# Linear attention and two mixtures on one core: the first mixture in pairs of experts, the first block of the second by plain products

## The chip, the cores and the metric

The kernel runs on one core of a Trainium2 chip. The metric is device time in microseconds (us) for one launch. TensorE (PE) multiplies, VectorE (DVE), ScalarE (ACT) and GpSimd (POOL) work on elements, and SyncE (SP) issues most of the DMAs. Every engine runs its own queue in order and waits on semaphores of the others.

## The reference, cut to what matters

Three layers follow one another on 2304 tokens of 512 numbers, in float32:

```python
def phi(x):                                  # linear attention, per head
    proj = x @ w_phi; proj -= abs(proj).max(-1, keepdims=True)
    return concatenate([exp(proj), exp(-proj)], -1)
x = phi(q) @ (phi(k).T @ v) / (phi(q) @ phi(k).sum(0) + 1e-6)

logits = x @ phi_moe                         # first mixture: 8 experts x 4 slots
slot_input = softmax(logits, over tokens).T @ x
slot_out[e] = relu(slot_input[e] @ w1[e]) @ w2[e]
x = softmax(logits, over slots) @ slot_out

P = exp(x @ w_gate - max)                    # second mixture, 8 experts
for _ in range(8):
    P /= P.sum(1) + 1e-9; P /= P.sum(0) + 1e-9; P *= N / E
out = sum(P[:, e] * (relu(x @ w1[e]) @ w2[e]) for e in range(8))
```

## The kernel before

All instructions are issued through `InOrder`, so the order of the program text is the order of each engine's queue, and every row of a trace shows line 51. Weights are loaded in units of 1 MB (four a first-mixture expert: `moe_w1` twice, `moe_w2` twice), SP issuing them in the order of the text into the pools `wa`, `wb` and `wq` (three units of 1 MB). A load waits until the tile that it overwrites has been read.

**First mixture.** For each expert e, `up(e, n)` (n = 0, 1; 16 matmuls each into `ph`) makes the hidden values of all slots, ACT writes `hid` from `ph`, `turn(e)` transposes it on PE (`pt`, two matmuls) and DVE writes the relu into `hz`, which POOL has cleared, and `down(e)` (16 matmuls) adds to `po`. The loop puts half the `up` of the next expert ahead of the `turn` and the other half behind it. Between them stand `slot_split` (DVE) and `slot_turn` (`pc` on PE, `ct` on ACT), which turn the slot weights of the tokens. After the loop `os` and `sot` are copied from `po` and `p_sot`.

**Second mixture.** The second layer's input is never formed: `make_stack` takes `sot` through `w1` (`ps`, `pr`, `st`), and `first_layer` makes the hidden values of a block of 256 tokens as `z` from `ct` and `st`. A block then multiplies a 2 x 2 split of the hidden values (a11, a12, a21, a22) with a 2 x 2 split of `w2` (b11, b12, b21, b22) by seven products of sums (`PRODUCTS`), twelve matmuls of 128x256 each, since each operand is split into a high part (`hh`, `w_hi`) and a low part (`hl`, `w_lo`), and `take` puts `x`, `y` or `z` into `xo`. ACT makes the high parts, DVE the low parts of a's (`hl_a`) and the sums s1 to s4 (`s`), POOL the low parts of the sums (`hl_s`) and those of the weights. Sums of weights are t1 to t4 (`w_sum`). In the trace `w_b` is an operand b11, b21 or b22, `w_t` one of t1 to t4. For expert 0 these operands are made during the loop of the first mixture (on ACT and DVE, from e = 5) and directly ahead of block 0 (on ACT and POOL). `sinkhorn` (`plog`, `gm`, `pgm`, `P`, `rs`, `cs`, `pcs`) makes P beside the products of expert 0: `SINK_0` and `SINK` say after which product k how many of its steps come. `pgm<-gm,ones` spreads the maximum over the partitions, `pcs` sums the columns.

The order within a block is: product k, `take`, after k = 2 the next block's `first_layer`, a step of `hidden` (the operands of the next block), weight work, steps of `sinkhorn`. The buffers of the sums (`s`) are three and go round, so `s4` waits until `hl_s` of `s1` has been read out of its buffer's earlier owner, and `s3` for `s2`'s.

## Time and profile before

| | us |
|---|---|
| median of 3 runs (lowest, highest) | 997.11 (996.86, 997.58) |
| the profiled execution's own time | 997.75 |
| its span, first to last instruction | 995.6 |
| PE busy in the span | 982.8 (99%) |
| DVE, POOL, ACT busy | 689.0, 595.0, 556.8 |
| DMA | 88.85 MB, 89 GB/s in the mean |

PE is busy 99% of the span, so time is won or lost in PE's own work and in the little that it waits. 2.15 us lie outside the span. The first mixture runs from 171 to 208 us, blocks 0 and 1 of the second from 215.67 to 238.86. The mean busy share says nothing on a single stage: DMA is near full from 175 to 222 us and almost idle in the second half.

### The profile page before, as it was taken

To read this page: it belongs to the slowest core of one execution; us is meant where nothing else is said; L and a number is where in the kernel's file an instruction comes from. 1 tells how busy PE (TensorE), PEld (TensorE's weight loads), DVE (VectorE), ACT (ScalarE), POOL (GpSimd) and SP (SyncE) were. 2 spreads that over 40 slices of the span, in tenths; PEclk is the share of its full clock that TensorE was granted. 3 is DMA by queue.
4 is the path that set the end of the run, shared out by engine and by line. 5 is a ranking of instruction groups with operands and counts; after the bars stand their busy time and mean duration, and the time that the engine had idled before them with its cause. 6 is when DMAs were issued, how large, how long until landed. Compare 5 with 4: busy or idle time off the path is not lost.

```text
span 995.6 us, 28041 instructions
## 1 busy us (share of the span) xinstructions
PE 982.8 (99%) x11698; PEld 934.5 (94%) x11698; DVE 689.0 (69%) x1359; ACT 556.8 (56%) x1018; POOL 595.0 (60%) x467
## 2 busy tenths in 40 slices
PE   8999999999999999999999999999999999999998
PEld 7899887469999999999999999999999999999998
DVE  6777776277886766676766776676676677667675
ACT  5576564266657666655564555555654655556452
POOL 2122221045678677867786688678677777687443
PEclk9999999999999999999999999999999999999999
DMA  8667577980003100310040005000300220001111
GB/s 259 209 213 235 158 261 271 392 327 2 1 1 128 44 1 2 129 43 1 1 164 8 1 2 170 1 2 28 143 2 1 76 95 1 2 1 36 51 44 64
DMA packets 28942, 88.85 MB, mean 89 GB/s; under 512 B 3856, under 2 KB 6800, under 8 KB 23056
## 3 DMA queue, kind: packets, MB, share of 16 engines
q1 hardware_dynamic: 19984, 68.05, 19.5%
q10 hardware_dynamic: 8640, 18.88, 5.9%
q8 instruction: 92, 1.51, 0.6%
q14 instruction: 34, 0.28, 0.1%
q0 software_dynamic: 192, 0.13, 0.1%
HBM read 82.33 MB, written 4.72 MB: 87 GB/s over the span
## 4 chain that ended last, share of the span: by engine, by line
PE 95%; DVE 1%; DMA 1%; ACT 1%; issue 1%; DVEq 0%; ACTq 0%
PE x L51 39%; PE y L51 20%; PE z L51 16%; PE kvacc L51 4%; PE num L51 4%; PE pq L51 2%; PE pk L51 2%; PE ut L51 2%; PE ps L51 2%; DMA moe_w<-in_moe_w 1%; PE ph L51 1%; PE po L51 1%; PE xt L51 1%; PE xl L51 1%; PE lg L51 0%
## 5 line engine op out<-in xcount | busy, mean ns | idle before, releaser
L51 POOL TENSOR_TENSOR hl_s<-s,hh_s 128x512 fp32r<-128x512 f32 x286 | 365.7, 1300 | 205.6 <-ACT hh_s L51 188.9
L51 PE MATMUL x<-w_t,hh_s 128*128 128x256 f32 x1152 | 204.9, 278 | 0.1
L51 ACT ACTIVATE hh_s<-s 128x512 fp32r<-128x512 f32 x287 | 174.7, 630 | 50.8 <-PE x L51 25.0
L51 ACT ACTIVATE r<-z 128x512 f32<-128x512 f32 x143 | 85.9, 601 | 163.7 <-PE z L51 163.1
L51 PEld LDWEIGHTS x<-w_t,hh_s 128*128 128x128 f32 x1152 | 173.5, 188 | 1.1 <-ACT xo L51 0.3
L51 DVE SCALAR_TENSOR_TENSOR xo<-x,P,xo 128x256 f32<-128x256 f32 x252 | 120.8, 479 | 69.2 <-PE x L51 68.6
L51 ACT ACTIVATE hh_a<-z 128x512 fp32r<-128x512 f32 x216 | 122.1, 600 | 72.8 <-DVE s L51 71.3
L51 PE MATMUL x<-w_t,hl_s 128*128 128x256 f32 x576 | 158.8, 277 | 0.0
L51 DVE SCALAR_TENSOR_TENSOR s<-z,r 128x512 f32<-128x512 f32 x143 | 98.0, 685 | 84.8 <-ACT hh_a L51 81.2
L51 DVE SCALAR_TENSOR_TENSOR hl_a<-z,hh_a 128x512 fp32r<-128x512 f32 x216 | 147.0, 681 | 2.7 <-ACT hh_a L51 2.7
L51 PEld LDWEIGHTS x<-w_t,hl_s 128*128 128x128 f32 x576 | 107.9, 188 | 0.0
L51 PE MATMUL z<-w_b,hh_a 128*128 128x256 f32 x576 | 102.4, 278 | 0.0
L51 PE MATMUL x<-w_t,hh_a 128*128 128x256 f32 x576 | 101.9, 277 | 0.0
L51 PE MATMUL y<-w_b,hh_s 128*128 128x256 f32 x576 | 101.8, 277 | 0.0
L51 PE MATMUL y<-w_t,hh_s 128*128 128x256 f32 x576 | 101.8, 276 | 0.0
L51 PE MATMUL x<-w_b,hh_a 128*128 128x256 f32 x576 | 101.5, 277 | 0.0
L51 DVE SCALAR_TENSOR_TENSOR s<-z,s 128x512 f32<-128x512 f32 x143 | 97.7, 683 | 3.7 <-POOL hl_s L51 2.2
L51 PEld LDWEIGHTS z<-w_b,hh_a 128*128 128x128 f32 x576 | 86.7, 188 | 2.9 <-issue 2.9
L51 PEld LDWEIGHTS x<-w_t,hh_a 128*128 128x128 f32 x576 | 86.8, 188 | 0.0
L51 PEld LDWEIGHTS y<-w_t,hh_s 128*128 128x128 f32 x576 | 86.9, 188 | 0.0
L51 PEld LDWEIGHTS y<-w_b,hh_s 128*128 128x128 f32 x576 | 86.8, 188 | 0.0
L51 PEld LDWEIGHTS x<-w_b,hh_a 128*128 128x128 f32 x576 | 86.7, 188 | 0.0
(206 smaller groups left out, 1983.5 us busy)
## 6 DMA issues: line engine op xcount, KB each, us to landing
moe_w<-in_moe_w SPq DMA_DIRECT2D x45, 1024.0 KB, 6.2
moe_w<-in_moe_w ACTq DMA_DIRECT2D x48, 256.0 KB, 3.6
moe_w<-in_moe_w ACTq DMA_DIRECT2D x12, 512.0 KB, 5.5
vs<-in_vb SPq DMA_DIRECT2D x20, 256.0 KB, 4.3
kt<-in_kT SPq DMA_DIRECT2D x18, 256.0 KB, 4.3
qt<-in_qT SPq DMA_DIRECT2D x18, 256.0 KB, 4.3
...
```

What stands on the lines that cost most here:

```text
L51: return lambda *args, **kwargs: self.tc.keep_in_program_order(make(*args, **kwargs))
```

## The change

- The pool `wq` becomes eight half units of 512 KB (`space`); `load_halves` places units 5, 6, 10 and 16 in them, so that one unit more is fetched ahead. The order of the later loads changes: the last units of the first mixture come ahead of the second mixture's.
- The first mixture goes by pairs of experts: four halves of `up`, one `turn` of four transposes, two `down`. The pool `mp` goes; `hid`, `hz` and `cst` take space in `const` and `early`. The load of `rep` is moved behind the loop.
- The operands of expert 0 for the second mixture are made no longer during the first mixture, but directly ahead of block 0 and, by `direct_work`, during it.
- Block 0 of expert 0 uses eight plain products (`DIRECT`: four results, two products each, of the a's with b11, b12, b21, b22) instead of the seven; b12 is an extra operand (`w0_b12`). Their results are copied to `xo` by ACT. `SINK_0` is moved to {0: 1, 5: 1, 6: 1, 7: 4}, so that the maximum is spread after the seventh product and the first `pcs` comes after the second product of block 1.

```diff
-    wq_cm = tc.tile_pool(name="wq", bufs=3, side="left", reuse_waits="tile")
+    wq_cm = tc.tile_pool(name="wq", bufs=1, side="left", reuse_waits="tile")
...
-    load_units(wq, 5, 6, 10)
+    space = [wq.tile([128, FF], F32, tag=f"h{n}", name=f"half{n}") for n in range(8)]
+
+    def load_halves(u, *where):
+        name, e, n = units[u]
+        unit_t[units[u]] = [space[m] for m in where]
+        for k, m in enumerate(where):
+            SP.dma_start(out=space[m], in_=a[name][e, :, n * 2048 + k * FF:n * 2048 + (k + 1) * FF])
+
+    load_halves(5, 0, 7)
+    load_halves(6, 1, 2)
+    load_halves(10, 3, 4)
     load_in_x(7)
+    load_halves(16, 5, 6)
...
-    for e in range(E):
-        if e + 1 < E:
-            up(e + 1, 0)
-        turn(e)
...
-        if e == 5:
-            w_begin(0)
-            w_hi(0, 0)
-            w_lo(0, 0, V)
-            w_sum(0, 0, V)
-        if e == 6:
-            w_lo(0, 3, V)
-            w_sum(0, 1, V)
-        if e == 7:
-            w_hi(0, 2)
-            w_lo(0, 1, V)
-            w_lo(0, 2, V)
-            w_sum(0, 3, V)
-            w_sum(0, 2, V)
...
+    for n in range(4):
+        up(n // 2, n % 2)
...
+    for p in range(E // 2):
+        a1, b1, more = 2 * p, 2 * p + 1, 2 * p + 2 < E
+        turn(p)
+        if p:
+            next(slot_turns)
+            next(slot_splits)
+        if more:
+            clear(p + 1)
+            up(a1 + 2, 0)
+            up(a1 + 2, 1)
+            if p == 0:
+                load_units(wb, 28)
+            up(b1 + 2, 0)
+            up(b1 + 2, 1)
...
+        if p == 2:
+            load_munits(3)
+        down(a1)
...
+        down(b1)
+        if p == 1:
+            load_units(wb, 31)
+            load_munits(1)
...
+    w_begin(0)
+    w_part(0, 0)
...
-            (G if i or name != "s1" else V).tensor_tensor(out=l, in0=s, in1=h.bitcast(F32), op=ALU.subtract)
+            G.tensor_tensor(out=l, in0=s, in1=h.bitcast(F32), op=ALU.subtract)
...
+    DIRECT = [
+        ("a11", 0, 0, 0), ("a11", "b12", 0, 1), ("a21", 0, 1, 0), ("a21", "b12", 1, 1),
+        ("a12", 1, 0, 0), ("a12", 5, 0, 1), ("a22", 1, 1, 0), ("a22", 5, 1, 1),
+    ]
...
+        if i == 0:
+            name, part, r, c = DIRECT[k]
+            if k < 4:
+                sums[r, c] = acc_tile(f"c{r}{c}")[:, 0:256]
+            h, l = hop[i, name]
+            accumulate(sums[r, c], h, l, wop[e, part], k < 4, k < 1 or k in (2, 4))
+            if k >= 4:
+                A.copy(out=xo[:, r, c * 256:(c + 1) * 256], in_=sums.pop((r, c)))
+            return
...
-    SINK_0 = {1: 1, 3: 1, 4: 1, 5: 1, 6: 3}
+    SINK_0 = {0: 1, 5: 1, 6: 1, 7: 4}
+
+    def direct_work(k):
+        if k == 1:
+            w_hi(0, 1)
+            w_hi(0, 5)
+            w_lo(0, 1)
+            w_sum(0, 1, V)
+            w_lo(0, 5, V)
+        if k == 2:
+            w_sum(0, 2, V)
+            w_part(0, 3)
+            w_sum(0, 3, V)
+        if k in (4, 5, 6):
+            w_part(0, {4: 2, 5: 4, 6: 6}[k])
```

PE in the first mixture before, experts 1 and 2, is one `up` half, a `turn`, the other half, a `down`:

```order
L51 MATMUL ph_3784<-moe_w_2_0_1379,sit_3676 32x256 x8
L51 MATMUL pt_3793<-ident,hid_3770 128x128 x2
L51 MATMUL ph_3784<-moe_w_2_1_1562,sit_3691 32x256 x8
L51 MATMUL po<-moe_w_1_0_3612,hz_3760 32x512 x4
L51 MATMUL po<-moe_w_1_1_0_3616,hz_3760 32x512 x2
L51 MATMUL po<-moe_w_1_1_1_3618,hz_3760 32x512 x2
```

After, PE has the second pair's transposes, both experts' `up` of the pair behind it, and then the pair's `down`:

```order
L51 MATMUL pt_3843<-ident,hids 128x128 x4
L51 MATMUL pc_3851<-ident,cst_3758 128x128 x4
L51 MATMUL ph_3864<-half_3615,sit_3686 32x256 x4
L51 MATMUL ph_3864<-half_3616,sit_3686 32x256 x4
L51 MATMUL ph_3864<-moe_w_4_1_3736,sit_3701 32x256 x8
L51 MATMUL ph_3882<-moe_w_5_0_2940,sit_3686 32x256 x8
L51 MATMUL ph_3882<-moe_w_5_1_3048,sit_3701 32x256 x8
L51 MATMUL po<-half_3613,hz_3777 32x512 x2
L51 MATMUL po<-half_3614,hz_3777 32x512 x2
L51 MATMUL po<-moe_w_2_1_2125,hz_3777 32x512 x4
L51 MATMUL po<-moe_w_3_0_2353,hz_3777 32x512 x4
L51 MATMUL po<-moe_w_3_1_2538,hz_3777 32x512 x4
```

The `turn` stands once for two experts, straight behind the `down` before it, and a half of `up` stands no longer between `hid` and it.

DVE from the maximum of the logits on, in block 0 before (`xo` is the result, `s_1_4314` and `s_1_4330` are s1 and s2 of block 1):

```order
L51 TENSOR_REDUCE gm<-plog 128x1
L51 SCALAR_TENSOR_TENSOR s_1_4314<-z_0_1_4304,r_1_4309 128x512
L51 SCALAR_TENSOR_TENSOR s_1_4330<-z_0_1_4304,s_1_4314 128x512
L51 SCALAR_TENSOR_TENSOR hl_a_1_4313<-z_0_1_4304,hh_a_1_4311 128x512
L51 TENSOR_REDUCE gm<-pgm 1x1
L51 TENSOR_TENSOR xo<-x_4240,xo 128x256
```

DVE after, at the same place (`t_4074` is t2, `w_b_4231` the low part of b22, the next two are `w_sum` 2 and 3, then s1, s2, two `hl_a` and s4 of block 1):

```order
L51 TENSOR_REDUCE gm<-plog 128x1
L51 TENSOR_TENSOR t_4074<-moe_w_0_0_3920,moe_w_0_1_3982 128x1024
L51 TENSOR_TENSOR w_b_4231<-moe_w_0_1_3982,w_b_4231 128x1024
L51 TENSOR_TENSOR moe_w_0_0_3920<-moe_w_0_0_3920,moe_w_0_1_3982 128x4x256
L51 TENSOR_TENSOR moe_w_0_1_3982<-moe_w_0_1_3982,t_4074 128x4x256
L51 SCALAR_TENSOR_TENSOR s_1_4282<-z_0_1_4272,r_1_4277 128x512
L51 SCALAR_TENSOR_TENSOR s_1_4297<-z_0_1_4272,s_1_4282 128x512
L51 SCALAR_TENSOR_TENSOR hl_a_1_4281<-z_0_1_4272,hh_a_1_4279 128x512
L51 SCALAR_TENSOR_TENSOR hl_a_1_4301<-z_0_1_4267,hh_a_1_4299 128x512
L51 SCALAR_TENSOR_TENSOR s_1_4330<-z_0_1_4267,s_1_4297 128x512
L51 TENSOR_REDUCE gm<-pgm 1x1
```

Four operations of 128x1024 moved in ahead of s1, and s4 ahead of the maximum over the partitions.

POOL after, from block 0 on (low parts of b21 and t1, then in turn `hl_s` of block 1 and a low part of a weight; before, all three low parts that POOL makes stand ahead of block 0's `hl_s`):

```order
L51 TENSOR_TENSOR w_b_4229<-moe_w_0_1_3982,w_b_4229 128x1024
L51 TENSOR_TENSOR w_t_4250<-moe_w_0_0_3920,w_t_4250 128x1024
L51 TENSOR_TENSOR hl_s_1_4304<-s_1_4282,hh_s_1_4302 128x512
L51 TENSOR_TENSOR w_t_4307<-t_4074,w_t_4307 128x1024
L51 TENSOR_TENSOR hl_s_1_4326<-s_1_4297,hh_s_1_4324 128x512
L51 TENSOR_TENSOR w_t_4332<-moe_w_0_0_3920,w_t_4332 128x1024
L51 TENSOR_TENSOR hl_s_1_4356<-s_1_4330,hh_s_1_4354 128x512
```

A low part of 128x1024 now stands between any two `hl_s` of block 1.

## Rows read from the trace of the kernel before

**Rows 1.** The page, chain of the work that ended last: share by engine.
```profile
PE 95%; DVE 1%; DMA 1%; ACT 1%; issue 1%; DVEq 0%; ACTq 0%
```

**Rows 2.** Windows: length, busy us and count of each engine; clock; DMA share; GB/s.
```profile
190.00:200.00 10.00, 10.00 (x124) 4.11 (x120) 2.33 (x9) 2.69 (x5) 0.62 (x2) 1.00 1.01 418
```

**Rows 3.** Timeline of PE, first mixture: start, us, engine, line, operation, count.
```profile
171.16 1.05 PE L51 MATMUL ph<-moe_w,sit 128*32 128x256 f32 x11
...
174.99 0.44 PE L51 MATMUL pt<-ident,hid 128*128 128x128 f32 x2
175.36 1.07 PE L51 MATMUL ph<-moe_w,sit 128*32 128x256 f32 x16
176.25 1.90 PE L51 MATMUL po<-moe_w,hz 128*32 128x512 f32 x16
177.97 1.05 PE L51 MATMUL ph<-moe_w,sit 128*32 128x256 f32 x16
...
207.56 1.16 PE L51 MATMUL p_sot<-sel,os 128*128 128x128 f32 x8
```

**Rows 4.** Timeline of ACT, first mixture and block 0 of the second.
```profile
180.51 0.47 ACT L51 ACTIVATE hid<-ph,rc 128x256 f32<-128x256 f32 x1 [2.96 <-PE ph L51]
...
209.72 1.99 ACT L51 CAST w_t<-moe_w 128x1024 fp32r<-128x1024 f32 x2 [0.26 <-DVE moe_w L51]
...
214.95 0.60 ACT L51 ACTIVATE hh_a<-z 128x512 fp32r<-128x512 f32 x1 [0.35 <-PE z L51]
...
215.92 1.09 ACT L51 ACTIVATE hh_a<-z 128x512 fp32r<-128x512 f32 x2
...
223.14 0.37 ACT L51 COPY xo<-y 128x256 f32<-128x256 f32 x1 [0.74 <-PE y L51]
...
227.97 0.42 ACT L51 ACTIVATE P<-P,gm 128x144 f32<-128x144 f32 x1
```

**Rows 5.** Timeline of PE, blocks 0 to 2 of the second mixture.
```profile
215.67 1.14 PE L51 MATMUL x<-w_b,hh_a 128*128 128x256 f32 x8
...
227.91 0.39 PE L51 MATMUL x<-w_b,hh_a 128*128 128x256 f32 x2
...
230.63 0.28 PE L51 MATMUL pcs<-cs,ones 128*128 128x8 f32 x2
...
232.26 1.11 PE L51 MATMUL z<-ct,st 128*128 128x256 f32 x8
233.21 0.40 PE L51 MATMUL y<-w_t,hh_s 128*128 128x256 f32 x2
...
234.62 0.40 PE L51 MATMUL x<-w_t,hh_s 128*128 128x256 f32 x2
...
238.86 0.40 PE L51 MATMUL x<-w_b,hh_a 128*128 128x256 f32 x2
```

**Rows 6.** Timeline of DVE: a sum of weights, s2 of block 1, the column sum.
```profile
203.77 1.22 DVE L51 TENSOR_TENSOR t<-moe_w,moe_w 128x1024 f32<-128x1024 f32 x1
...
223.23 0.69 DVE L51 SCALAR_TENSOR_TENSOR s<-z,s 128x512 f32<-128x512 f32 x1
...
229.45 0.43 DVE L51 TENSOR_REDUCE cs<-P 128x8 f32<-128x144 f32 x1
```

**Rows 7.** Timeline of POOL, blocks 0 to 2 of the second mixture.
```profile
218.33 1.29 POOL L51 TENSOR_TENSOR hl_s<-s,hh_s 128x512 fp32r<-128x512 f32 x1 [0.41 <-ACT hh_s L51]
220.21 1.60 POOL L51 TENSOR_TENSOR hl_s<-s,hh_s 128x512 fp32r<-128x512 f32 x1 [0.59 <-ACT hh_s L51]
...
242.13 2.40 POOL L51 TENSOR_TENSOR w_b<-moe_w,w_b 128x1024 fp32r<-128x1024 f32 x1
```

**Rows 8.** Timeline of DVE, operations with two inputs in SBUF.
```profile
219.98 0.68 DVE L51 TENSOR_TENSOR hl_s<-s,hh_s 128x512 fp32r<-128x512 f32 x1
...
231.67 0.31 DVE L51 TENSOR_TENSOR P<-P,cs 128x144 f32<-128x144 f32 x1
...
242.72 1.98 DVE L51 TENSOR_TENSOR P<-P,cs 128x144 f32<-128x144 f32 x1
```

More of the change, by code (lines that the diff above doesn't have):

```diff
@@ L785, in up, with clear, turn @@
         if n == 1:
[L786 to L803 removed]
+            A.activation(out=hids[:, e % 2], in_=ph_t.pop(e)[:, 0:256], func=AF.Copy, scale=counts[:, 0:1])
+    def clear(p):
+        where, tag = (const, "si") if p % 2 else (early, "xT")
+        pair = where.tile([128, 2, 2, 4, NS], F32, tag=tag, name=f"hz{p}", bufs=1)
+        hz_t[2 * p], hz_t[2 * p + 1] = pair[:, 0], pair[:, 1]
+        G.memset(pair, 0.0)
+    def turn(p):
+        pt = mm(f"pt{p}")
+        for e in (2 * p, 2 * p + 1):
+            for n in range(2):
+                o = (2 * (e % 2) + n) * 128
+                PE.transpose(pt[:, o:o + 128], hids[:, e % 2, n * 128:(n + 1) * 128], ident)
+        for e in (2 * p, 2 * p + 1):
+            V.tensor_scalar_max(
+                hz_t[e][:, :, :, e * SPE:(e + 1) * SPE].rearrange("p n g j -> p (n g) j"),
+                pt[:, e % 2 * 256:(e % 2 + 1) * 256].rearrange("p (c j) -> p c j", j=NS)[:, :, e * SPE:(e + 1) * SPE],
+                0.0,
+            )
     def down(e):
@@ L943, in tile_kernel @@
+    rep = const.tile([128, 512], F32R, tag="x4", name="rep", bufs=1)[:, 120:376].rearrange("p (a c) -> p a c", a=2)
+    for g in range(4):
+        r = slice(32 * g, 32 * g + 32)
+        G.dma_start(out=rep[r], in_=a["rep"][r, g * 256:(g + 1) * 256].rearrange("p (a c) -> p a c", a=2))
     os = const.tile([128, DM], F32, tag="si", name="os", bufs=1)
@@ L946, in tile_kernel @@
     next(slot_turns)
+    next(slot_splits)
     ps = mm("p_sot")
@@ L952, in tile_kernel @@
         A.copy(out=sot[:, 2 * h:2 * h + 2].rearrange("p c j -> p (c j)"), in_=ps[:, h * 256:(h + 1) * 256])
-    keep_busy(True, 4)
-    mp_cm.__exit__(None, None, None)
+    next(slot_turns)
+    keep_busy(True, 2)
+    wq_cm.__exit__(None, None, None)
+    early_cm.__exit__(None, None, None)
+    cl1 = ctx.enter_context(tc.tile_pool(name="cl1", bufs=1, side="left", reuse_waits="tile"))
+    w_begin(0)
+    w_part(0, 0)
     wk1_cm.__exit__(None, None, None)
@@ L1153, in hidden, with accumulate @@
         yield
+    DIRECT = [
+        ("a11", 0, 0, 0), ("a11", "b12", 0, 1), ("a21", 0, 1, 0), ("a21", "b12", 1, 1),
+        ("a12", 1, 0, 0), ("a12", 5, 0, 1), ("a22", 1, 1, 0), ("a22", 5, 1, 1),
+    ]
+    def accumulate(ps, h, l, w, fresh, later):
+        terms = [(c, x, part) for c in range(KH) for x, part in ((h, 0), (h, 1), (l, 0))]
+        if later:
+            terms.sort(key=lambda term: 2 * (term[1] is l) + term[2])
+        for n, (c, x, part) in enumerate(terms):
+            PE.matmul(ps, x[:, c], w[:, part, c], start=fresh and n == 0, stop=n == len(terms) - 1, skip_group_check=True)
     def product(i, k):
         e, blk = blocks[i]
+        if i == 0:
[7 more added lines that the diff above has]
+            return
         a, _, to = PRODUCTS[k]
-        if (i, to) not in sums:
+        fresh = (i, to) not in sums
+        if fresh:
             sums[i, to] = acc_tile(f"{to}_{i}")[:, 0:256]
-            fresh = True
-        else:
-            fresh = False
         h, l = hop.pop((i, a))
-        w = wop[e, k]
-        ps = sums[i, to]
-        terms = [(c, x, part) for c in range(KH) for x, part in ((h, 0), (h, 1), (l, 0))]
-        if i == 0 and k < 3:
-            terms.sort(key=lambda term: term[1] is l)
-        for n, (c, x, part) in enumerate(terms):
-            PE.matmul(ps, x[:, c], w[:, part, c], start=fresh and n == 0, stop=n == len(terms) - 1, skip_group_check=True)
+        accumulate(sums[i, to], h, l, wop[e, k], fresh, False)
         if blk == NBLK - 1:
@@ L1206, in tile_kernel @@
     gmt = cp.tile([128, 2], F32, name="gm")
[L1207 to L1212 removed]
+    extra = cl2.tile([128, 2, KH, 256], F32R, tag=f"wo{NW - 1}", name="w0_b12", bufs=1)
+    wop[0, "b12"] = extra
+    A.copy(out=extra[:, 0], in_=wsrc[0]["t3"])
     def gate():
@@ L1217, in tile_kernel @@
     stacks = {0: make_stack(0, gate)}
+    V.tensor_tensor(out=extra[:, 1], in0=wsrc[0]["t3"], in1=extra[:, 0].bitcast(F32), op=ALU.subtract)
+    w_sum(0, 0, V)
     next(sink)
@@ L1235, in tile_kernel @@
             w_begin(e + 1)
-        for k in range(7):
+        for k in range(7 if i else 8):
             product(i, k)
@@ L1242, in tile_kernel @@
                 spread_stack(stacks[e + 1], e + 1)
-            if k == 2 and i + 1 < len(blocks):
+            if k == (2 if i else 3) and i + 1 < len(blocks):
                 first_layer(i + 1, 1)
```

132 lines of the change are left out of this document (40 added, 92 removed).

## The prediction

> **What bounds the kernel now.** I read the chain of the work that ended last first: 95% of it is PE [rows 1], so a change counts only where it takes PE work away, adds some, or makes PE wait. Then the table by stages: in the first mixture the DMA engines are full, 1.01 of their time at 418 GB/s, while PE is busy all 10.00 us of the stretch; ACT and POOL have room (2.69 and 0.62 us); the granted clock is 1.00 [rows 2]. So loads run level with PE there but don't hold it. Then the timelines of PE, ACT, DVE and POOL between 170 and 245 us, since order of instructions from the third block of the second mixture on is unchanged.
>
> **First mixture: what goes away.** Before, from the first `ph` at 171.16 to `p_sot` at 207.56, PE needs 36.40 us [rows 3]. In these rows half an `up` takes 0.89 (175.36 to 176.25), a `down` 1.72 (176.25 to 177.97), the two transposes of one expert 0.37 (174.99 to 175.36) [rows 3]. After, four transposes stand together; I take 0.6 for them, between 0.37 and twice that. Three halves and a code gap brought PE to 174.99; a fourth half first puts the end of both experts' `up` at 175.9. Then the first `turn` has to wait for ACT, which no up hides now: `hid` is 0.47 long [rows 4] and each of two handovers some 0.2, an estimate, together 0.85, so 176.7. The two filler transposes of `keep_busy` fall into this wait and cost nothing. A pair of experts is 0.6 + 4 x 0.89 + 2 x 1.72 = 7.6 us, and the second and third pair carry four `pc` transposes more, at the price of the other transposes about 0.45: 7.6 + 8.05 + 8.05 brings 200.4. The last pair has no `up` left: 0.6 + 0.45 + 3.44, 204.9, and 0.6 for copying `os`: `p_sot` at 205.5. That is **2.0 us less**. Bounds: 1.2, if each of four pair turns loses another 0.2 to a handover, and 2.5, if the gap in the fetch of code at the start closes. The prework on `w_b`, `w_t` and the sums of block 0 that leaves this stage frees ACT and DVE only, which PE did not wait for. The loads come as halves and further ahead; cover is the same full DMA, and no half is issued behind a wait that PE's last uses of a unit do not already set.
>
> From `p_sot` to the first product is the same chain as before, 207.56 to 215.67, 8.11 us [rows 3, 5]. So the first product starts at 213.6. From here I count from that start, T.
>
> **Block 0: one product more.** Before, blocks 0 and 1 took 215.67 to 238.86, 23.19 us, waits included [rows 5]. A product of twelve matmuls costs 1.41 (233.21 to 234.62) or 1.36 (227.91 to 230.63 are two); the eight matmuls of `z` 0.95 [rows 5]. I take 1.385. Eight products instead of seven: 1.4 more by itself.
>
> **Block 0: what now lies beside it.** The operands that were prepared under the first mixture are now made during the block, on ACT, POOL and DVE, and that decides the case. The first `hh_a` runs 0.72 ahead of T, two cost 1.09, a cast of 1024 some 1.0, a copy of a result 0.37 at most [rows 4]. So ACT ends four `hh_a` at T+1.4, `w_b21` at 2.3, `w_b22` 3.3, `w_t1` 4.2. DVE: a sum of 1024 is 1.22, a `s` 0.69 [rows 6]; it makes four `hl_a` to T+2.9 and the maximum of the logits to 3.4, and then meets four subtractions or sums of 1024 with both inputs in SBUF: `t`, the low part of `w_b22`, and `w_sum` 2 and 3; behind them in its queue stand `s1` and `s2` of block 1. POOL meanwhile makes low parts of 2.40 [rows 7].
>
> The rows that decide this lie elsewhere in the second mixture. `P<-P,cs`, two SBUF inputs, takes 0.31 us at 231.67, where POOL is idle, but 1.98 us at 242.72, where POOL has been at a low part since 242.13 for 2.40; it ends 0.17 after POOL's [rows 7, 8]. The reverse: DVE's `hl_s` at 219.98 came first, and POOL's at 220.21 was 1.60 instead of 1.29 [rows 7, 8]. I read that whichever of the two starts first holds the other off until it ends. The Trainium skill, "SBUF — State Buffer", section "Who interferes with whom", says the same of a DVE instruction with two SBUF inputs beside a GpSimd one that reads SBUF: the second fully blocks. If the two shared bandwidth, as the 0.31 alone could also be read, the four sums would each be longer by 0.31/0.68 of 1.13, 2.1 us in all; some 0.4 of it would be slack, and the sum below would be 999.6 and not 1002.1.
>
> With the block: POOL holds from 2.4 to 4.75 (`w_b21`); `t` goes 4.75 to 5.85; POOL, waiting since 4.75, takes `w_t1` to 8.2; DVE's low part of `w_b22` 8.2 to 9.4, the two sums to 11.6, `s1` to 12.25. PE's fourth product ends at 5.7, `z` at 6.7, the fifth product at 8.1; the sixth needs the low part of `w_b22` from its fifth matmul and **waits 0.9**, to 10.4; the seventh ends at 11.8. Then stands the ones matmul of `pgm`, which spreads the maximum: its value comes from DVE behind `s4`, and `s4` waits for the release of `s1` by POOL. `hh_s1` 12.9, `hl_s1` (1.29, [rows 7]) 14.25, `s4` and the maximum 15.2: PE, there at 11.8, **waits 3.4**. The eighth product ends at 16.9, two products of block 1 at 19.7. The column sum `pcs` comes next: POOL low part of `t2` to 16.6, `hl_s2` to 17.85, DVE `s3`, `hl_a22` and the negative maximum to 19.2, then exp to column sum, 227.97 to 229.88 or 1.9 us [rows 4, 6], with another 0.95 held off by POOL's `hl_s4` at the row normalisation: 22.1. PE **waits 2.5**. From `pcs` to block 2 the rows give 8.23 at the slower pace [rows 5], 8.0 at my mean: T+30.2.
>
> So blocks 0 and 1 cost 30.2 instead of 23.2: **7.0 us more**, of which 1.4 is the eighth product and 6.8 the three waits, less some 1.2 of waits that the 23.19 contained. If DVE kept its turn for all four sums ahead of POOL's `w_t1`, `s1` would end at 9.9 and the sum be 28.8; if POOL went on ahead of DVE, 33.7. I take the middle case, one each in turn, since the instruction that waited at 242.72 got in directly behind the one that held it.
>
> **The sum.** -2.0 + 7.0 = +5.0 on the profiled execution, 997.75: 1002.75. That execution lies 0.64 above the median of the runs, 997.11, so the forecast is **1002.1**. Nothing is late further on: all later blocks have the same code. Products in block 1 to 8 alternate between the two paces, as 1.36 ahead of the `pcs` at 230.63 and 1.41 behind it [rows 5]; if the alternation begins on the other foot, that is 0.4 a block, at most +0.7 or -1.0 in all, taken as nothing.
>
> **Rivals.**
> Not slower: POOL's low parts don't hold DVE's sums off. Then `s1` is there before the copy of the fifth product, `s4` follows `hl_s1` at T+11, the maximum is out at 12.0 and PE, there at 10.9, waits 1.1; `pcs` is out at 18.0 instead of 16.5, and block 2 starts at T+26.0. That is +2.8 - 2.0, 997.9; with both sides only slowed, as above, 999.6. For it: no row has a sum of 1024 on DVE beside a low part on POOL; against: the short `P` and the two `hl_s` [rows 7, 8] all behave as if there were one port for both. It decides from the point where the four sums end later than about T+8.3, 0.4 after they would alone. Chance 0.17.
> Faster: also the waits at the ones matmul and at `pcs` don't open, since ACT's copies of results are hardly behind. Then blocks 0 and 1 are 23.4, the change is -1.8, up to -2.3 with the gap in the code gone: 994.8 to 995.4. Against: both waits follow from the lengths above with no port in dispute. Chance 0.08.
> Slower still: POOL is first throughout, 33.7: 1005.6. Chance 0.05.
> The change does not do what it says: the loads hold the first mixture, since halves come slower than units. The DMA has no room there [rows 2]; if it loses the gain of 2.0, 1004. That no half lies in the full stretch leaves it open. Chance 0.04. The Trainium skill, "DMA: Bandwidth & Descriptors", section "Measured (HBM→SBUF, 128 partitions, SWDGE, issued from GpSimd)", wants at least 1 MiB in a transfer, and so speaks against halves; no run here shows its price. Worked out from the same section's 0.95 us for 64 KB, an estimate, four transfers more would add 3.8 us if nothing overlapped.
>
> **How the numbers follow.** Forecast 0.66, its own range 1000.2 (DVE keeps its turn, gain 2.5) to 1003.6 (gain 1.2 and the slow pace). The range for 8 in 10 must reach into the first rival: 997.5 to 1003.6 leaves out the faster rival, a part of the first, and what lies above. 0.2%, 2.0 us, is about what a measurement of this kernel can tell from no change: faster is below 995.1, slower above 999.1. Faster 0.08, same 0.18 (nearly all of the first rival and a rest of the second), slower 0.74.
>
> **What would show it.** `p_sot` at 205.5 shows the first mixture. In block 0, DVE's `t` of over 2 us and a low part of `w_b22` of over 2 us show the block; PE idle ahead of the ones matmul of 3.4 and ahead of `pcs` of 2.5 shows where it lands. If DVE's sums are 1.2 each and PE waits 1 us at the ones matmul, the first rival has it. PE waiting for a `half` in the first mixture would show the loads.

## The result and the profile after

The changed kernel takes 1005.94 us, the median of six runs (1003.19 to 1007.04); the kernel before, in six runs beside it, 997.92 (996.86 to 1000.13). The ratio is 1.0072, 95% interval 1.0053 to 1.0092; the same two kernels against each other a second time (12 and 32 runs) gave 1.0053 (1.0037 to 1.0070). Slower, as forecast: by 7.2 us by the ratio (8.0 by the medians), and by 5.3 (7.0) the second time. The forecast said 5.0, from a base of 997.11, and its range ended at 1003.6, 2.3 us short.

The profiled execution took 1007.04, the longest of the six, its span 1005.3 us. PE is busy 983.3 us, against 982.8 before: what came in is nearly all waiting. In the chain of the work that ended last, PE's share falls by one point, `issue` (time in which an engine waited for nothing that the profile shows) and transfers rise from 1 to 2%, and POOL shows (page of the changed kernel; [rows 1] is its counterpart):

```profile
PE 94%; issue 2%; DMA 2%; POOL 1%; DVE 1%; ACT 0%; POOLq 0%; DVEq 0%; ACTq 0%
```

I cut every trace at the same six points of PE's timeline. The two kernels were profiled six and five times in all (the later ones are among the experiments below); the means of those:

| us | before, profiled run of [rows 3, 5] | after, profiled run | before, mean of 5 | after, mean of 6 | difference of means | forecast |
|---|---|---|---|---|---|---|
| span start to first `ph` (attention) | 171.16 | 174.87 | 172.19 | 173.75 | +1.6 | 0 |
| first `ph` to `p_sot` | 36.40 | 32.94 | 35.73 | 33.13 | -2.6 | -2.0 |
| `p_sot` to first product (T) | 8.10 | 9.03 | 8.10 | 8.86 | +0.8 | 0 |
| T to first product of block 2 | 23.19 | 30.32 | 23.12 | 30.24 | +7.1 | +7.0 |
| block 2 to the first `ps` of expert 1 | 66.41 | 66.41 | 66.40 | 66.40 | 0 | 0 |
| from there to the end of PE's work | 686.61 | 687.81 | 686.62 | 687.80 | +1.2 | 0 |

What lies behind the end of PE's work, up to the measured time, is 5.68 us after and 5.86 before in the mean, 0.2 less; with it the rows add up, but for rounding, to the 7.8 us between the mean times of the profiled executions.

**First mixture.** PE's timeline of the changed kernel; columns as in [rows 3]. The four halves, the filler, the first `turn`, and the ends of the later pairs:

```profile
174.87 2.80 PE L51 MATMUL ph<-moe_w,sit 128*32 128x256 f32 x48
177.48 1.05 PE L51 MATMUL ph<-half,sit 128*32 128x256 f32 x16
178.46 0.44 PE L51 MATMUL busy<-ident 128*128 128x128 f32 x2
178.73 0.83 PE L51 MATMUL pt<-ident,hids 128*128 128x128 f32 x4
...
186.52 0.66 PE L51 MATMUL pt<-ident,hids 128*128 128x128 f32 x4
...
194.56 0.65 PE L51 MATMUL pt<-ident,hids 128*128 128x128 f32 x4
...
202.61 0.66 PE L51 MATMUL pt<-ident,hids 128*128 128x128 f32 x4
...
207.81 1.16 PE L51 MATMUL p_sot<-sel,os 128*128 128x128 f32 x8
...
212.03 1.07 PE L51 MATMUL ps<-moe_w,sot 128*32 128x256 f32 x16 [0.86 <-DMA moe_w<-in_moe_w]
```

Four halves end 3.59 after the first `ph`; in [rows 3] three halves and the gap took 3.83 (3.03 to 3.04, without a gap, in the other four profiles of before). The wait for `hids` is 0.27, and no line waits for a `half`. The last line, behind `p_sot`, is new: the second W1 unit of the second mixture hasn't landed, and PE stands 0.86.

**Blocks 0 and 1.** The lines of PE that carry a wait, and the first of block 2 ([rows 5] is the counterpart):

```profile
226.07 0.38 PE L51 MATMUL c<-w_b,hh_a 128*128 128x256 f32 x1 [0.90 <-DVE w_b L51]
...
231.87 0.38 PE L51 MATMUL pgm<-gm,ones 1*128 1x1 f32 x2 [2.76 <-DVE gm L51]
...
238.85 0.36 PE L51 MATMUL pcs<-cs,ones 128*128 128x8 f32 x2 [2.30 <-DVE cs L51]
...
247.16 0.40 PE L51 MATMUL x<-w_b,hh_a 128*128 128x256 f32 x2
```

DVE and POOL beside them (timelines; columns as in [rows 6, 7]):

```profile
219.85 0.30 DVE L51 TENSOR_REDUCE gm<-plog 128x1 f32<-128x144 f32 x1
220.06 2.62 DVE L51 TENSOR_TENSOR t<-moe_w,moe_w 128x1024 f32<-128x1024 f32 x1
222.60 3.42 DVE L51 TENSOR_TENSOR w_b<-moe_w,w_b 128x1024 fp32r<-128x1024 f32 x1
225.94 1.21 DVE L51 TENSOR_TENSOR moe_w<-moe_w,moe_w 128x1024 f32<-128x1024 f32 x1
```

```profile
219.19 2.41 POOL L51 TENSOR_TENSOR w_b<-moe_w,w_b 128x1024 fp32r<-128x1024 f32 x1 [5.70 <-ACT w_b L51]
221.55 3.39 POOL L51 TENSOR_TENSOR w_t<-moe_w,w_t 128x1024 fp32r<-128x1024 f32 x1
```

POOL's 2.41 ends at 221.60; `t`, begun at 220.06, ends at 222.68, so it did its 1.2 only then; POOL's next, begun at 221.55, ends at 224.94, 2.26 behind `t`; DVE's next, begun at 222.60, ends at 226.02, 1.08 behind that. One at a time, in turns. Where POOL has nothing, the same sum on DVE is 1.21 (last line of DVE's).

### The profile page after: what moved, and what is told of

The parts are those of the page before. It is cut to its first block, busy times and chain, and to the rows that moved or that the text cites. A ratio compares the mean times of both kernels' runs of the same rounds, so it can differ in the third digit from the quotient of the medians.

```text
span 1005.3 us, 28048 instructions
## 1 busy us (share of the span) xinstructions
PE 983.3 (98%) x11710; PEld 937.9 (93%) x11710; DVE 687.8 (68%) x1350; ACT 555.1 (55%) x1014; POOL 598.8 (60%) x463
## 4 chain that ended last, share of the span: by engine, by line
PE 94%; issue 2%; DMA 2%; POOL 1%; DVE 1%; ACT 0%; POOLq 0%; DVEq 0%; ACTq 0%
PE x L51 39%; PE y L51 19%; PE z L51 16%; PE kvacc L51 4%; PE num L51 3%; PE pq L51 2%; PE pk L51 2%; PE ut L51 2%; DMA moe_w<-in_moe_w 2%; PE ps L51 1%; PE ph L51 1%; PE po L51 1%; PE xt L51 1%; PE xl L51 1%; POOL w_t L51 1%
## 5 line engine op out<-in xcount | busy, mean ns | idle before, releaser
L51 PE MATMUL x<-w_t,hh_s 128*128 128x256 f32 x1136 | 202.5, 278 | 0.0
```

The lines of the kernel that those rows point to most:

```text
L51: return lambda *args, **kwargs: self.tc.keep_in_program_order(make(*args, **kwargs))
```

## The experiments

Kernels run together share runs of before. All times below are medians of runs, ratios are to before with 95% intervals, and lengths of stages come from one profile each.

| kernel | us | ratio | first `ph` | to `p_sot` | to T | blocks 0 and 1 | block 2 to expert 1 | to the end |
|---|---|---|---|---|---|---|---|---|
| a_again (changed kernel) | 1005.85 | 1.0053 (1.0037 to 1.0070) | 175.03 | 32.94 | 9.14 | 30.30 | 66.40 | 687.81 |
| b_again (before) | 999.61 | 1.0001 (0.9980 to 1.0023) | 171.89 | 35.88 | 8.09 | 23.12 | 66.41 | 686.62 |
| t1_later | 1005.01 | 1.0051 (1.0031 to 1.0072) | 171.06 | 32.94 | 9.92 | 30.49 | 66.38 | 687.81 |
| late_sink | 1002.06 | 1.0028 (1.0010 to 1.0045) | 172.10 | 33.51 | 8.23 | 29.25 | 66.42 | 685.61 |
| half7_last | 1001.62 | 1.0046 (1.0029 to 1.0062) | 170.07 | 32.95 | 8.11 | 30.86 | 66.41 | 685.73 |
| low_dve | 1006.83 | 1.0093 (1.0080 to 1.0106) | 174.93 | 32.94 | 9.35 | 31.84 | 66.65 | 685.76 |
| low_dve_h7 | 1005.01 | 1.0077 (1.0055 to 1.0098) | 174.77 | 32.94 | 8.10 | 32.13 | 66.65 | 689.06 |
| low_dve2 | 1000.74 | 1.0024 (1.0002 to 1.0047) | 171.30 | 32.94 | 8.23 | 28.15 | 66.39 | 685.74 |
| low_dve3 | 1002.46 | 1.0041 (1.0022 to 1.0059) | 171.37 | 32.94 | 8.10 | 27.54 | 67.93 | 685.79 |

**The two kernels again, unaltered.** The changed kernel:

> The changed kernel once more, with nothing altered. In the first execution its first `ph` came at 174.87 us, 3.71 us later than before the change, although PE's, SP's and ACT's queues up to there read alike; PE waited 4.6 us ahead of `kvacc` with nothing in the profile to wait for (`issue`), 1.7 before. Theory 1 (the length of the attention stage scatters from execution to execution): the first `ph` comes anywhere between 171 and 175 here, and the median lies 4.5 to 5.5 us above the kernel before. Theory 2 (the change itself lengthened the attention stage, by where code or buffers lie): 174.5 to 175.2 again, `issue` ahead of `kvacc` over 4 us, and the median 7 to 8.5 us above. Both: blocks 0 and 1 of the second mixture take 30.2 to 30.4 us again, which depends on no earlier stage.

The kernel before:

> The kernel before once more, with nothing altered. Theory 1 (scatter): its first `ph` comes at another time than 171.16, by up to 4 us, with another length of `issue` ahead of `kvacc`. Theory 2 (the change lengthened the stage): 171.0 to 171.4 again, `issue` under 2 us.

Blocks 0 and 1 repeat to 0.02 us in the one and 0.07 in the other: the 7 us belong to the program. So do the last 687.81 and 686.62. The first `ph` decided nothing here: 175.03 and a median 7.0 above before are what theory 2 said of the changed kernel, though its `issue` ahead of `kvacc` was 3.6 and not over 4; 171.89, with 2.6 of `issue`, lies outside what theory 2 said of before. That is taken up last.

**Is it the hold-off? POOL's low part of `w_t1` moved away from DVE's sums (t1_later).**

```diff
@@ direct_work, k == 2
             w_sum(0, 2, V)
-            w_part(0, 3)
             w_sum(0, 3, V)
@@ k in (4, 5, 6)
+        if k == 5:
+            w_part(0, 3)
```

> The changed kernel with one operand, t1, made later: ACT's cast and POOL's low part of it come behind the fifth operand of block 0, so that POOL has only the low part of `w_b21` beside DVE's four sums of two inputs in SBUF. Theory (one holds the other off): DVE's `t` is still 2.5 to 2.7 us, but the low part of `w_b22` 1.2 instead of 3.4; PE's wait for it goes (0.9 to 0), `s1` comes 2.3 us earlier, and blocks 0 and 1 take 28.5 to 29.2 us, 1.1 to 1.8 less than 30.3. Rival (DVE's sums are slow for another reason, such as loads that land in the same memory): `w_b22` stays over 2 us and nothing is gained.

DVE of this kernel, the same two operations as above and the later row normalisation, then POOL beside the latter:

```profile
217.10 2.61 DVE L51 TENSOR_TENSOR t<-moe_w,moe_w 128x1024 f32<-128x1024 f32 x1
219.64 1.21 DVE L51 TENSOR_TENSOR w_b<-moe_w,w_b 128x1024 fp32r<-128x1024 f32 x1
...
232.51 1.65 DVE L51 TENSOR_TENSOR P<-P,rs 128x144 f32<-128x144 f32 x1
```

```profile
229.29 4.71 POOL L51 TENSOR_TENSOR w_t<-moe_w,w_t 128x1024 fp32r<-128x1024 f32 x2
```

The low part of `w_b22` falls from 3.42 to 1.21, and PE's 0.90 is gone; `t`, which still meets POOL's `w_b21`, stays at 2.61. That shows the mechanism for that instruction: nothing else about it changed. The time does not follow; the stage took 30.49 where 28.5 to 29.2 was expected. PE's wait at the ones matmul is 1.73 instead of 2.76, but POOL now has two low parts in a row just where `P<-P,rs` wants its turn, and PE stands 3.37 at `pcs` instead of 2.30. Behind that idle time the granted clock falls (windows of this kernel: stretch, length; busy us and count of PE, PEld, DVE, ACT, POOL; clock; DMA share; GB/s):

```profile
232.00:236.00 4.00, 1.25 (x9) 1.28 (x10) 3.62 (x8) 0.09 (x1) 4.00 (x3) 0.95 0.27 47
236.00:240.00 4.00, 4.00 (x25) 4.00 (x25) 2.56 (x4) 1.57 (x3) 2.93 (x2) 0.63 0.89 289
```

In that stretch a product takes 2.21 instead of 1.50 and `z` 1.71 instead of 0.94: 1.5 us. The expected gain, 0.9 and 1.0 at two waits, was made and given back, 1.1 at the next wait and 1.5 to the clock.

**Is it only where the gating stands? Its matmuls later, `pcs` in an accumulator bank (late_sink).**

```diff
-            pg = z_tile(0, f"pcs{it}") if it < 7 else acc_tile(f"pcs{it}")
+            pg = z_tile(0, f"pcs{it}") if 0 < it < 7 else acc_tile(f"pcs{it}")
-    SINK_0 = {0: 1, 5: 1, 6: 1, 7: 4}
+    SINK_0 = {0: 1, 5: 1, 7: 5}
+    SINK_1 = {4: 3, 5: 2}
-                for _ in range((SINK if blk else SINK_0).get(k, 0)):
+                for _ in range((SINK if blk > 1 else SINK_1 if blk else SINK_0).get(k, 0)):
```

> The changed kernel with two matmuls of the gating moved later in PE's queue: the ones matmul of `pgm` behind the eighth product (was: the seventh), the first `pcs` behind the fifth product of block 1 (was: the second). Theory (the waits of 2.8 and 2.3 us are a matter of what stands behind them in PE's queue, since the operands of the next products are ready earlier): the wait at the ones matmul shrinks to about 1.4, that at `pcs` to under 0.3, blocks 0 and 1 take 26.3 to 27 us instead of 30.3, and the whole is 3.3 to 4 us shorter than the changed kernel. Rival (late operands, `hl_s` and the low parts on POOL, bind as well): PE then waits at the third product of block 1 or later for POOL, and the gain is under 1.5 us.

PE's lines with a wait in blocks 0 and 1 of this kernel:

```profile
223.06 0.39 PE L51 MATMUL c<-w_b,hh_a 128*128 128x256 f32 x1 [0.66 <-DVE w_b L51]
...
228.87 0.38 PE L51 MATMUL pgm<-gm,ones 1*128 1x1 f32 x2 [1.34 <-DVE gm L51]
...
233.64 0.50 PE L51 MATMUL x<-w_t,hh_s 128*128 128x256 f32 x2 [1.36 <-ACT xo L51]
...
238.78 0.38 PE L51 MATMUL x<-w_t,hl_s 128*128 128x256 f32 x1 [0.86 <-POOL hl_s L51]
```

The 2.30 at `pcs` is gone, and 1.36 behind ACT and 0.86 behind POOL stand where it was: 29.25, a gain of 1.07, in size what the rival said. But only the 0.86 is the wait for a low part that it named. The 1.36 is for ACT's copy of block 1's first result out of the bank to which PE's third product adds (ACT's timeline):

```profile
232.92 0.42 ACT L51 ACTIVATE P<-P,gm 128x144 f32<-128x144 f32 x1
233.24 0.35 ACT L51 COPY xo<-x 128x256 f32<-128x256 f32 x1
```

ACT works without a pause of more than 0.04 from 225.91 to the end of this copy, 233.59, on casts of weights, high parts and copies, and the gating's exponential stands right ahead of the copy. So not the gating alone is late: ACT's row and POOL's are too, and the gating's matmuls were only the first to meet it. The lower ratio is owed to more than this stage: it also has 2.2 less at the end (below).

**The wait behind `p_sot`: half units in the order in which their space comes free (half7_last).**

```diff
-    load_halves(5, 0, 7)
-    load_halves(6, 1, 2)
-    load_halves(10, 3, 4)
+    load_halves(5, 0, 1)
+    load_halves(6, 2, 3)
+    load_halves(10, 4, 5)
     load_in_x(7)
-    load_halves(16, 5, 6)
+    load_halves(16, 6, 7)
```

> The changed kernel with the eight half units taken in another order: unit 5 goes to spaces 0 and 1, 6 to 2 and 3, 10 to 4 and 5, 16 to 6 and 7, so that space 7, for whose earlier contents SP waited until 167.7 us, is written last and not second. Theory (this one wait stood at the head of SP's queue and put off all later loads; DMA moved 68 GB/s from 165 to 170): DMA is busy in the 10 us ahead of the first `ph`, the loads end about 3 us earlier, PE's wait of 0.86 for `moe2_w1` ahead of the second `ps` goes, and from `p_sot` to the first product it is 8.0 to 8.2 us instead of 9.0. Rival (the loads are bound by the DMA rate throughout): the wait stays within 0.3 of 0.86. Both: the first mixture from `ph` to `p_sot` stays at 32.9 and blocks 0 and 1 at 30.3; the whole is at most 1 us less.

What SP issued (timeline of SP's queue: start, duration of the group, what is loaded, count) and the window from 165 to 170, first in the changed kernel:

```profile
167.73 2.93 SPq L51 DMA_DIRECT2D half<-in_moe_w  x5
```

```profile
165.00:170.00 5.00, 4.93 (x95) 3.44 (x90) 3.26 (x14) 0.93 (x4) 0.50 (x1) 1.00 0.26 68
```

Then here:

```profile
158.07 5.28 SPq L51 DMA_DIRECT2D half<-in_moe_w  x5
163.44 1.43 SPq L51 DMA_DIRECT2D moe_w<-in_moe_w  x2
```

```profile
165.00:170.00 5.00, 4.78 (x93) 3.81 (x93) 2.44 (x12) 0.73 (x4) 0.75 (x2) 1.00 0.94 323
```

In the changed kernel space 7 is wanted by the second half loaded. SP, which issues in order, stands behind what was in that space, for 8.7 us, until 167.73 (its wait is for DVE's `x`, ahead of the first mixture), and the DMA engines are busy 0.26 of their time, where it is 0.94 here and 0.97 in the kernel before. The stretch behind it, 1.01 full from 175 on, has no room to make that up, so the last units land later. With the order put right, `p_sot` to T is 8.11, as before the change (8.10 to 8.23 in the four kernels that have this order, 8.38 to 9.14 in the six profiles of the changed kernel). Blocks 0 and 1 didn't gain: they are 0.5 longer, with the clock at half from the wait at the ones matmul on (windows of this kernel).

```profile
224.00:228.00 4.00, 1.86 (x8) 1.84 (x9) 1.96 (x4) 4.00 (x8) 4.00 (x3) 0.75 0.00 0
228.00:232.00 4.00, 4.00 (x21) 4.00 (x21) 2.42 (x6) 2.41 (x5) 4.00 (x3) 0.50 0.00 0
```

**The low parts on DVE instead of POOL (low_dve).** An operation of 1024 is 1.2 on DVE and 2.4 on POOL, so with one at a time the pair of them should be done sooner. All of POOL's low parts of weights go to DVE, two of them behind block 0's eighth product; the last weight moves into block 1, and the gating stands earlier.

```diff
-    SINK_0 = {0: 1, 5: 1, 6: 1, 7: 4}
+    SINK_0 = {0: 1, 4: 1, 5: 2, 6: 3}
@@ direct_work
         if k == 1:
             w_hi(0, 1)
-            w_hi(0, 5)
-            w_lo(0, 1)
             w_sum(0, 1, V)
+            w_hi(0, 2)
+            w_lo(0, 1, V)
+            w_sum(0, 2, V)
+            w_hi(0, 5)
             w_lo(0, 5, V)
         if k == 2:
-            w_sum(0, 2, V)
-            w_part(0, 3)
-            w_sum(0, 3, V)
-        if k in (4, 5, 6):
-            w_part(0, {4: 2, 5: 4, 6: 6}[k])
+            w_hi(0, 3)
+            w_lo(0, 2, V)
+        if k == 3:
+            w_hi(0, 4)
+        if k == 7:
+            w_lo(0, 3, V)
+            w_lo(0, 4, V)
@@ the loop over blocks
-        if blk == 1 and more:
+        if blk == 1 and more and e:
             w_begin(e + 1)
+            if i == 1 and k == 0:
+                w_sum(0, 3, V)
+                w_part(0, 6, V)
+                w_begin(1)
```

> The changed kernel with the low parts of all weights of block 0 and 1 made by DVE instead of POOL (1.2 us instead of 2.4 each), so that POOL has only the four `hl_s` of block 1; the fourth sum and the operand t4 are made during block 1; the transposition of the maximum comes behind the fifth product, the ones matmul and the exponential behind the sixth, the row and column sums behind the seventh. Theory (the 7.1 us that blocks 0 and 1 lost come from POOL's and DVE's turns at one port, and from the chain s1, `hl_s`, s4, maximum that stands behind it): with the turns worked through by the lengths of the trace, blocks 0 and 1 take 24.5 to 25.5 us instead of 30.3, PE waits under 1 us at each of the two gating matmuls, and 1 to 2 us for the operands of the fourth product of block 1 and for `xo`. Rival (the eight products and the copies of results by ACT bind, not POOL and DVE): 28 us or more.

PE's lines with a wait in blocks 0 and 1, and two windows of this kernel:

```profile
226.87 0.27 PE L51 MATMUL pgm<-ident,gm 128*1 128x128 f32 x1 [1.18 <-ACT xo L51]
...
240.71 1.22 PE L51 MATMUL z<-ct,st 128*128 128x256 f32 x4 [4.08 <-DVE cs L51]
```

```profile
236.00:240.00 4.00, 0.63 (x6) 0.43 (x4) 2.89 (x3) 1.82 (x3) 0.00 (x0) 0.86 0.50 147
240.00:244.00 4.00, 3.29 (x15) 3.29 (x16) 2.98 (x9) 0.60 (x1) 0.00 (x0) 0.50 0.92 328
```

The waits of 0.90, 2.76 and 2.30 are gone. But `z` of block 2 uses the bank that `pcs` stands in; its reader on DVE was queued behind the low parts and the sum, and PE stood 4.08 (that reader, in DVE's timeline):

```profile
240.50 0.16 DVE L51 TENSOR_SCALAR cs<-pcs 128x8 f32<-128x8 f32 x1
```

Again the clock went to half behind it, which cost some 2.4 us. The expectation for the stage, 24.5 to 25.5, fell, by a wait that I had not looked for; 31.84 is in the rival's range (28 or more), but not by what the rival named. With the half units in order as well, `p_sot` to T was 8.10 and the same wait stayed (3.96), so of the two gains that were to add up only one came:

> Both changes of the other two kernels in one: half units in the order of half7_last, low parts on DVE as in low_dve. Theory: both gains add, 0.8 to 1 us from `p_sot` to the first product and about 5 us in blocks 0 and 1. With `ph` to `p_sot` at 32.9, `p_sot` to the first product at 8.1 and blocks 0 and 1 at 25 it would be 1.7 us shorter than the kernel before in these three stretches (32.9 + 8.1 + 25.0 = 66.0 against 36.4 + 8.1 + 23.2 = 67.7), less or more by the pace of the products later on, which moved by up to 1.2 us between kernels; so a ratio between 0.997 and 1.000 to the kernel before. Rival: earlier loads collide with something else, and nothing is gained beside low_dve.

**That bank and its reader apart (low_dve2).** To the last kernel, `pcs` as in late_sink and one cast later:

```diff
-            pg = z_tile(0, f"pcs{it}") if it < 7 else acc_tile(f"pcs{it}")
+            pg = z_tile(0, f"pcs{it}") if 0 < it < 7 else acc_tile(f"pcs{it}")
-        if k == 3:
+        if k == 5:
             w_hi(0, 4)
```

> After with the low parts of block 0's weights on VectorE, the gating's steps earlier (1, 1, 2 and 3 behind products 1, 5, 6 and 7), the W1 unit last in the half units' queue, and, against the kernel before it in this series, the first column-sum matmul (pcs) in an accumulator bank instead of z's bank, with the cast of the fifth weight two products earlier. Theory (the 4.0 us for which z of block 2 waited on VectorE's reader of pcs, and the half clock of 236 to 248 us that came with it, are all that kept blocks 0 and 1 at 32): they take 24.5 to 26 us; with 32.9 from ph to p_sot and 8.1 from there to the first product that is 65.5 to 67 against 67.7 before, and the time is 0.997 to 1.001 of before's, with the scatter of the attention stage on top. Rival (operands of VectorE's row bind, so that the next reader in its queue takes the place of cs): z's wait goes, another of 2 us or more shows in block 1 or 2, blocks 0 and 1 (to the first product of block 2) stay above 28.5 us, and the ratio is 1.004 to 1.009.

The expectation calls the move of that cast, the fifth weight's, earlier; the edit makes it two products later. Blocks 0 and 1 fall from 32.13 to 28.15, above the theory's range and below the rival's, and so is the ratio. The wait of 3.96 and the half clock behind it are gone, but PE now stands 0.59 and 1.90 at products of block 1, behind readers of result banks on ACT and DVE. On ACT stands the next queue (ACT's timeline of this kernel):

```profile
232.85 1.05 ACT L51 CAST w_t<-moe_w 128x1024 fp32r<-128x1024 f32 x1 [4.16 <-DVE moe_w L51]
```

**The queue behind that cast (low_dve3).**

```diff
             if i == 1 and k == 0:
                 w_sum(0, 3, V)
-                w_part(0, 6, V)
+            if i == 1 and k == 2:
+                w_hi(0, 6)
+            if i == 1 and k == 3:
+                w_lo(0, 6, V)
                 w_begin(1)
```

> The same kernel as the one before it in this series, with ScalarE's cast of the last weight of expert 0 two products later in block 1 and its low part three products later: behind ScalarE's r22 and first high part of block 2, instead of ahead of them. In the kernel before, ScalarE stood 4.16 us in front of that cast, behind VectorE's sum of the weight, with r22 and the reader of the x bank queued behind it, and TensorE then waited 0.6 us for that reader and 1.9 us for VectorE's, whose queue had slipped. Theory (the queue behind the cast is the cause): both waits go, blocks 0 and 1 take 25.3 to 26.3 us instead of 28.15, the steps from ph to the first product of block 2 sum to 66.4 to 67.4 against 67.7 of before, and the ratio is 0.997 to 1.001. Rival (VectorE is full in block 1 with the low parts that it took over, 3.74 us for two beside POOL, and would be late whatever ScalarE does): the 1.9 us stay or move to the next product, blocks 0 and 1 stay at 27.5 us or more, and the ratio is 1.002 to 1.004.

PE's one line with a wait in block 1:

```profile
238.44 0.50 PE L51 MATMUL x<-w_t,hh_a 128*128 128x256 f32 x2 [2.04 <-DVE xo L51]
```

The rival held: ACT's stand is gone, and DVE is as late as it was (2.04 against 1.9), being full with the low parts that it took over. Then the clock fell, at a cost of 1.5 us in block 2 (67.93 against 66.4; window of this kernel):

```profile
240.00:244.00 4.00, 4.00 (x23) 4.00 (x23) 1.75 (x4) 2.89 (x6) 3.12 (x3) 0.59 0.58 213
```

None of these kernels beats the one before. In the stage, moving the work about gave 27.54 at best, and 30.5 to 32.1 in four kernels of seven; 23.1, with the work done ahead in the first mixture, wasn't reached.

**Scatter or program? More profiles of both kernels, unaltered.** The first three:

> The changed kernel unaltered, a third profile, for the first ph alone. It stood at 174.87 and 175.03 us in the two profiles of it so far, at 171.16 and 171.89 in the two of before, with code of the attention stage that is the same in both, and PE idle 11.1 and 10.6 against 7.7 and 8.6 us ahead of it. Theory (executions scatter, whatever the kernel): of this profile and the next at least one has its first ph below 173.5, with PE idle below 9 us ahead of it. Rival (something in the changed program, such as where its code lies, makes the attention stage longer in every execution): both at 174.3 to 175.6, with 10 us idle or more.

> The changed kernel unaltered, a fourth profile, as the run before. Theory (scatter): first ph below 173.5 us here or in the third profile. Rival (the changed program): 174.3 to 175.6 in both. The steps behind ph as before under either: 32.9 from ph to p_sot, 8.9 to 9.2 to the first product T, 30.2 to 30.4 for blocks 0 and 1.

> The kernel before unaltered, a third profile. Theory (scatter): first ph anywhere from 170 to 175.5 us; one above 173.5 would show it by itself. Rival (the program): 170.5 to 172.5. The steps behind it: 35.9 to 36.4, 8.1 and 23.1 to 23.2 us.

And four more:

> The kernel before unaltered, a fourth profile, for the first ph: 171.16, 171.89 and 170.62 us so far. Theory (scatter of executions, the same for both kernels): of this and the next at least one lies above the lowest of the changed kernel, 172.39, or one of the changed kernel's next two below 171.9. Rival (the changed program's attention stage is longer by itself): this and the next again at 170.5 to 172.0.

> The changed kernel unaltered, a fifth profile; first ph at 174.87, 175.03, 173.94 and 172.39 so far. Theory (scatter): this or the next reaches below 171.9, into the range of before. Rival (the program): both above 172.3, so that six of six lie above every one of before's.

> The kernel before unaltered, a fifth profile, as the fourth: above 172.39 by the theory in this or in that, 170.5 to 172.0 in both by the rival.

> The changed kernel unaltered, a sixth profile, as the fifth: below 171.9 by the theory in this or in that, above 172.3 in both by the rival. From the first product of block 2 to the end 754.2 us, 1.2 more than before, in both, if the pace of the products belongs to the program.

| profile, us | before: first `ph` | to `p_sot` | time | after: first `ph` | to `p_sot` | time |
|---|---|---|---|---|---|---|
| on record | 171.16 | 36.40 | 997.75 | 174.87 | 32.94 | 1007.04 |
| again | 171.89 | 35.88 | 997.87 | 175.03 | 32.94 | 1007.32 |
| look2 | 170.62 | 35.73 | 996.49 | 173.94 | 33.51 | 1005.99 |
| look3 | 172.00 | 35.42 | 997.50 | 172.39 | 32.95 | 1004.54 |
| look4 | 175.29 | 35.21 | 1000.48 | 172.81 | 32.95 | 1004.60 |
| look5 | | | | 173.44 | 33.51 | 1005.68 |

The profile look4 of before stands at 175.29, above all of the changed kernel's: the first `ph` scatters between executions, by 4.7 us in before and 2.6 in the changed kernel. Of what was expected, scatter held for the changed kernel's third and fourth profile (172.39, with PE idle 8.3 us ahead of it) and for before's fourth and fifth (175.29); the rival held for the changed kernel's fifth and sixth (both above 172.3), and before's third (170.62) fits both. What scatters is PE's waiting in the attention stage, 7.7 us over all its lines in the profile of before on record and 11.1 in that of after, most of the difference in `issue` ahead of `kvacc`. That this is PE waiting for its own code, as the prediction has it of the gap at the start, no row shows. PE's waits up to the first `ph`, summed by what was waited for (us in total, times, longest), of before, then of after:

```profile
PE kvacc L51 <- issue: 1.7, 2, 1.3
...
PE kvacc L51 <- ACT phik L51: 0.9, 1, 0.9
```

```profile
PE kvacc L51 <- issue: 4.6, 3, 1.8
PE kvacc L51 <- ACT phik L51: 1.4, 1, 1.4
```

Whether 1.6 us of mean is owed to the program as well can't be said from six and five values that spread by 2.6 and 4.7. Three experiments above have the changed kernel's text up to block 0, and their first `ph` is at 171.06, 172.10 and 174.93 (t1_later, late_sink, low_dve): with them nine profiles reach down into the range of before, and the mean difference is 1.2. The length to the end does not scatter: 687.80 to 687.81 in six profiles of after, 686.61 to 686.63 in five of before. It belongs to the program.

## Why the forecast was right in kind and short in size

The steps that failed are three terms of the sum put at nothing: the stretch from `p_sot` to T (+0.8), the pace of the later products (+1.2) and the attention stage ahead of the first `ph` (+1.6, cause open). The first mixture was mis-sized the other way.

**Blocks 0 and 1: right, the total nearly to the digit.** Counted from T (216.84 in the profiled execution), `t` ends at 5.84 where 5.85 was forecast, POOL's `w_t1` at 8.1 (8.2), the low part of `w_b22` at 9.2 (9.4), `s1` at 12.05 (12.25); PE's waits are 0.90, 2.76 and 2.30 for 0.9, 3.4 and 2.5, and block 2 begins at 30.32 (30.2). That the total fits so well is in part luck: the wait at the ones matmul is 0.6 shorter because PE came to it 0.5 later, the first product alone having taken 1.71 and not 1.385. The choice of the middle case, one each in turn, was the right one: DVE's low part waited for POOL's `w_t1`, and POOL's for `t`. The Trainium skill, "SBUF — State Buffer", section "Who interferes with whom", says that a DVE instruction with two SBUF inputs contends with a GpSimd instruction that reads SBUF, and that the ports which they share are an exclusive lock. The trace agrees (2.62 and 3.42 for 1.21, 3.39 for 2.4), and t1_later turned 3.42 into 1.21 by moving POOL's instruction alone. The rivals in which they share or DVE keeps its turn fell. What the forecast did not see is how little hangs on the single wait: each experiment that took one away found the next within 1 to 4 us.

**First mixture: sign right, mis-sized.** In the execution on record the gain was 3.46, not 2.0. From the first `turn` on the steps stood: pairs of 7.79, 8.04 and 8.05 for 7.6, 8.05 and 8.05, the last with the copy of `os` 5.20 for 5.09. The error lies ahead of it: the step "Three halves and a code gap brought PE to 174.99; a fourth half first puts the end of both experts' `up` at 175.9" kept the gap, which wasn't there (3.59 for 4.74, or 1.15), and the wait for `hid` was 0.27 for 0.85. The gap wasn't closed by the change: it belongs to the one execution on record and shows in no other profile of before. So 36.40 was the longest of five executions of before, and against their mean the gain is 2.6. Nor is it so that PE "did not wait for" DVE in that stage: in before, on record,

```profile
205.15 1.92 PE L51 MATMUL po<-moe_w,hz 128*32 128x512 f32 x16 [0.33 <-DVE hz L51]
```

and 0.45 and 0.60 in two of the other four profiles; after the change this wait is gone.

**From `p_sot` to T: the step failed.** "No half is issued behind a wait that PE's last uses of a unit do not already set" is wrong: the second transfer asks for space 7, for which SP has to stand 8.7 us. Forecast 0, measured 0.93 in the execution on record, 0.8 in the mean; half7_last takes it back in full. It was the order of the queue and not the size of the pieces, since half7_last has the same eight pieces. So the rule of the Trainium skill, "DMA: Bandwidth & Descriptors", section "Measured (HBM→SBUF, 128 partitions, SWDGE, issued from GpSimd)", which wants 1 MiB in a transfer and which I weighed there, doesn't account for this loss; what the size of the pieces costs by itself no run shows.

**The pace: outside its bounds.** Taken as nothing, with +0.7 or -1.0 as its bounds, it is +1.2. It shows in the stretch from 950 to 970, clock 1.00 and PE busy throughout, as fewer matmuls, 172 in the changed kernel against 179 in before and in half7_last, 1.41 us a product against 1.36 (windows of the changed kernel, then of before):

```profile
950.00:970.00 20.00, 20.00 (x172) 20.00 (x171) 13.46 (x27) 9.48 (x18) 9.10 (x8) 1.00 0.11 38
```

```profile
950.00:970.00 20.00, 20.00 (x179) 20.00 (x178) 13.74 (x28) 9.79 (x18) 9.35 (x8) 1.00 0.16 54
```

Between kernels the last part ranged from 685.6 to 689.1 us. The choice of bounds failed, since the alternation was read block by block and the long stretches at one pace were not. What sets the pace I can't say: no experiment changed it by intent.

**The base and the attention stage.** The stages from the first `ph` on, by the means, give -2.6 + 0.8 + 7.1 + 1.2 = 6.5 us, where +5.0 was forecast. The rest of the miss can't be laid to them: the median of before was 997.92 and not 997.11 beside it, and the profiled executions of after stood 1.6 us later at the first `ph`, which the forecast put at 0 and of which it is open whether the program or the scatter makes it. The range took one execution's attention stage as fixed, where the later runs of before alone cover several us (994.9 to 1002.2 in 17 runs beside low_dve2). The low end reached far into the first rival, the high end only to the sum of two of its own terms.

The rivals: no hold-off (997.9 or 999.6) and faster fell in DVE's and POOL's rows; POOL first throughout (33.7 for the blocks) fell at 30.3, and that its 1005.6 comes nearest to the measured time is chance; loads holding the first mixture fell there, since no line waits for a `half`, but its transfers came back one stage later.
